# An FFT filter with a top-k FFN on one Trainium2 core: DRAM input and output padded to 128 partitions, one transfer per half

## The chip, the cores and the metric

The kernel runs on one core of one Trainium2 chip. The metric is device time in microseconds (us), the median of several executions. The core has five instruction streams: TensorE (PE in the profile, its weight loads PEld), VectorE (DVE), ScalarE (ACT), GpSimd (POOL) and SyncE (SP). In this kernel SyncE issues all plain transfers between DRAM and SBUF, and GpSimd the indirect ones (gather and scatter by a list of row numbers); 16 DMA engines carry both.

## The reference, cut to what matters

```python
# x: (8, 3136, 256) float32; filt_r, filt_i: (1569, 256); capacity C = 128
X = np.fft.rfft(x, axis=1)
y = np.fft.irfft(X * (filt_r + 1j * filt_i)[None], n=3136, axis=1)   # global filter over the sequence
scores = np.einsum('bsd,d->bs', y, w_gate)
out = y.copy()
for b in range(8):
    top = np.argpartition(-scores[b], C)[:C]          # the C tokens with the highest score
    ye = np.maximum(y[b, top] @ w1, 0.0) @ w2         # 256 -> 1024 -> 256
    out[b, top] = y[b, top] + sigmoid(scores[b, top])[:, None] * ye
```

## The kernel before

The sequence of S = 3136 tokens is split as 98 x 32, and the FFT of one batch is done in stages of matrix products. The **outer** stage reads X, a tile of [128 partitions, 2 halves, 2, 16, 128 channels], 32 KB per partition. A half is 128 of the 256 channels. The 98 rows of 32 tokens lie on partitions 0 to 48 and 64 to 112 (NH = 49 rows each), 16 tokens in each of the two blocks k of a partition. Compute instructions run over partitions 0 to 112 (113 of them); rows 49 to 63 carry nothing of use, and partitions 113 to 127 are touched by none.

For batch `b_in` the outer stage takes eight chunks of 32 channels: `fold` (L489) forms sum and difference of the two blocks, or the chunk goes in unfolded; `amm` (L500) multiplies on TensorE; `tout` (L505, VectorE) transposes the result into UU. The **inner** stage does seven steps per batch: `zmm` (L376), the products with the filter `pmul`, `qdir`, `qmul` (L384, L391, L387), `vmm` (L400), copies back to UU (L408, L410) and the scores (`gmul`, `gsum`, `gate`: L435, L441, L416). Then the outer stage of the *next* round transforms the chunk of `b_out` back (`tin` L479, `imm` or `ymm` L531, L563) and writes it into the same place of X, either with one ACT copy (`yout`, L567) or with two copies and two `join`s (L537, L541), of which the first writes the block k = 0 and the second k = 1.

**X exists once.** Round t of `outer` works on b_out = t - 1 and b_in = t + 1: a chunk of X is read as input of b_in and then overwritten with the output of b_out. After the fourth and the eighth chunk `stored` (L571) has SyncE store the half (`store_rows`), and then `load` (L584) fetches the same half for two batches on. Batch 0 is loaded in quarters (`load_first`, L602). The transfers are these:

- a store of a half (L579, L580): four transfers of 48 partitions x 16 tokens x 512 bytes, one per block k (called h there) and per half of the partitions (g), and after each two a transfer of 2 partitions for row 48;
- a load of a half (L594, L595): one of partition 112 alone, cut into 16 pieces of 1 KB, then one of partitions 0 to 111, 16 KB each. `kernel()` lays the input out in DRAM for this.

The output in DRAM is (8, 3136, 256) in the order of the tokens; a half of a token is 512 bytes and a token 1 KB.

**Selection and FFN.** `select` finds the 128 highest scores of a batch by a search in steps on ACT, TensorE and VectorE; it sends the scores to a DRAM scratch (`scr`, L672) and back spread over partitions (`R`, L698). Its step `c12` (L876) writes the row numbers `idx` for the gather from the output (`gather`, L970). `ffn` multiplies (L976 transposes, L999 and L1006 up, L1039 down), adds (`gated`, L1042) and writes back (`scatter`, L1046). w1 and w2 are loaded late (L923, L925). The FFN of the last batches is the end of the kernel.

**Order.** Every instruction stream runs in the order written out by hand in ORDER: a list of all steps, issued one after the other, so each engine takes its instructions in that order. The change leaves the list as it is.

Of the kernel before, what the change touches and what calls it, by code (L numbers as in the profile page):

```python
# [9 lines left out]
F32 = mybir.dt.float32  # L10
# [4 lines left out]
ALU = mybir.AluOpType  # L15
# [36 lines left out]
def _tables(C):  # L52
# [25 lines left out]
    k = (k1[:, None, :] + N1 * np.arange(K2)[None, :, None]).reshape(2 * K2, L)  # L78
    rows = np.minimum(k, S - k)

    cst = np.zeros((128, NCONST), f)
    p = np.arange(128)
# [11 lines left out]
    j = p // NCHK  # L94
    cst[:, _COLS["nb0"]] = (2.0**31 - j * STEPS[0] + STEPS[3] / 2)[:, None]
    cst[:, _COLS["nb1"]] = (-j * STEPS[4] + STEPS[7] / 2)[:, None]
    for r in range(8):
        d = j * (STEPS[r] - (STEPS[r + 1] if r % 4 < 3 else 0)) - (STEPS[r] / 2 if r % 4 == 3 else 0)
# [3 lines left out]
    cst[:, _COLS["half7"]] = NCHK * W7 - 2 * C + 1  # L102
    cst[:, _COLS["pick"]] = (p[:, None] % NCHK == p[None, :] % NCHK) & (p[:, None] < NROW * NCHK)
    cst[:, _COLS["block"]] = p[:, None] // NCHK == np.arange(NROW)[None, :]
    cst[:, _COLS["slot"]] = p[:, None]
    cst[:, _COLS["row"]] = N2 * p[:, None]


    tf = np.stack([tf[h, :, :, :, :, h] for h in range(2)]).reshape(128, L, 64)
# [119 lines left out]
        a=['vzaaazav', 'zazyzava', 'yyavyavv', 'avyvyaya', 'vvzayzza', 'vvavvyay', 'vaayvyvz', 'vayavyay'],  # L229
# [25 lines left out]
def kernel(  # L255
# [7 lines left out]
    nc = tc.nc  # L263
# [11 lines left out]
    HD = D // 2  # L275
    CW = 16
    DW = 2 * CW
    DS = D + 1
    oi = out.rearrange("b (h a g n) d -> b g a h n d", h=2, g=2, n=NG)
    of = out.rearrange("b s d -> (b s) d")  # L280

    c_sb = const.tile([128, NCONST], F32, name="c_sb")
    cc = {k: c_sb[:, v] for k, v in _COLS.items()}
# [8 lines left out]
    X = const.tile([128, 2, 2, NG, HD], F32, name="X")  # L292
    wg_sb = const.tile([128, D], F32, name="wg_sb")
    idx_sb = const.tile([128, B], I32, name="idx_sb")
    g_sb = const.tile([128, B], F32, name="g_sb")
# [161 lines left out]
    halves = [c_sb[:, _COLS["wi"].start + NH * k:_COLS["wi"].start + NH * k + 64] for k in range(2)]  # L457
# [115 lines left out]
            stored(c, hx)  # L573

    def store_rows(b, x):
        d = slice(x * HD, x * HD + HD)
        for h in range(2):
            for g in range(2):
                nc.sync.dma_start(out=oi[b, g, :48, h, :, d], in_=X[64 * g:64 * g + 48, x, h])  # L579
            nc.sync.dma_start(out=oi[b, :, 48, h, :, d], in_=X[48::64, x, h])  # L580

    XM = 2 * 112 * 4096

    def load(when, b, h, xy, bias=0.0):  # L584
        n = NCH // 2
        where[:] = "ld", b, h
        if b < B:
            keys = [("x", h, c, g) for c in range(h * n, h * n + n) for g in range(2)]
            to = X[:, h].rearrange("p k n d -> p (k n d)")
            main = x[b, :XM].rearrange("(h p e) -> h p e", h=2, p=112)  # L590
            ends = x[b, XM:].rearrange("(r h e) -> h r e", h=2, r=16)

            def fetch():
                nc.sync.dma_start(out=to[112:113].rearrange("p (r e) -> p r e", r=16), in_=ends[h:h + 1])  # L594
                nc.sync.dma_start(out=to[:112], in_=main[h])  # L595

            op(when, "sp", 7.15, fetch, [], keys, lat=2.2, bias=bias, tag="load")

    x_flat = X.rearrange("p x k n d -> p (x k n d)")
    x_first = x_flat.rearrange("p (q k n d) -> p q k n d", q=4, k=2, n=NG)  # L600

    def load_first():  # L602
        main = x[0, :XM].rearrange("(q p e) -> q p e", q=4, p=112)
        ends = x[0, XM:].rearrange("(r q e) -> q r e", q=4, r=16)

        def quarter(q):
            to = x_flat[:, 2048 * q:2048 * q + 2048]
            nc.sync.dma_start(out=to[112:113].rearrange("p (r e) -> p r e", r=16), in_=ends[q:q + 1])
            nc.sync.dma_start(out=to[:112], in_=main[q])

        for q in range(4):
            keys = [("x", q // 2, 4 * q + c, g) for c in range(4) for g in range(2)]
            op(XQ[q], "sp", 3.7, lambda q=q: quarter(q), [], keys, lat=2)

    def select(T0, b, st):
# [27 lines left out]
        def s1():  # L643
            st["Dt"] = Dt = sel.tile([N1, 2 * N2 + 1], F32, name="Dt")
            sp = st["sp"]
            nc.vector.tensor_reduce(out=Dt[:, N2:2 * N2], in_=sp[:N1, :, 192:224].rearrange("p g n -> p n g"), op=ALU.add, axis=AX.X)
            nc.vector.tensor_copy(out=Dt[:, 2 * N2:], in_=cc["row"][:N1])


        def s2():  # L650
# [23 lines left out]
        def s6p():  # L674

            st["ks"] = ks = flt.tile([128, 2, 2 * D], F32, name="q", bufs=BUFS["q"])[:NROW * NCHK, :, :W7]
            nc.gpsimd.memset(ks[96:], 0.0)
            nc.gpsimd.memset(ks[96:, :, W7 - N2:], -2.0**32)

        def s6q(ph):  # L680
            nc.vector.tensor_tensor(out=st["ks"][:N1, ph].rearrange("p (i n) -> p i n", n=N2), op=ALU.mult,
                                    in0=st["kf"][:, ph:ph + 1].to_broadcast([N1, NROW, N2]),
                                    in1=cc["block"][:N1, :, None].to_broadcast([N1, NROW, N2]))
# [189 lines left out]
        def c12():  # L873
            rp, col = st["rp"], st["col"]
            st["idx"] = idx = idx_sb[:, b:b + 1]
            nc.vector.tensor_scalar(out=idx[:C], in0=col[:C], scalar1=rp[:C, 2 * N2:2 * N2 + 1], scalar2=float(b * S),  # L876
                                    op0=ALU.add, op1=ALU.add)
            jk = sel.tile([128, N2], F32, name="jk")
            st["g"] = g = g_sb[:, b:b + 1]
            nc.vector.scalar_tensor_tensor(out=jk[:C], in0=cc["iota"][:C, :N2], scalar=col[:C],  # L880
                                           in1=rp[:C, N2:2 * N2], op0=ALU.is_equal, op1=ALU.mult, accum_out=g[:C])
# [77 lines left out]
    def ffn(TG, T, TE, bs, sts, plain=False):  # L959

        g = len(bs)
        where[:] = "ff", bs[0]
        one = plain or bs[0] == B - 1
        xe = [xes[b][0] for b in bs]
# [2 lines left out]
        ftile = bank  # L967

        def gather(j):
            nc.gpsimd.indirect_dma_start(out=xe[j][:C], out_offset=None, in_=of[:(bs[j] + 1) * S],  # L970
                                         in_offset=bass.IndirectOffsetOnAxis(ap=sts[bs[j]]["idx"][:C, 0:1], axis=0))

        def turn(j, ring):
# [69 lines left out]
                                           op0=ALU.mult, op1=ALU.add)  # L1043

        def scatter(j):
            nc.gpsimd.indirect_dma_start(out=of[:(bs[j] + 1) * S],  # L1046
                                         out_offset=bass.IndirectOffsetOnAxis(ap=sts[bs[j]]["idx"][:C, 0:1], axis=0),
                                         in_=xe[j][:C], in_offset=None)

# [16 lines left out]
        for f in fs:  # L1066
# [4 lines left out]
            r = XT + ([("w1",)] if one else [("wl", n) for n in range(4)])  # L1071
            op(t, "pe", cost, lambda f=f, ring=ring: up(f, 0, ring), [*r, ("ups",), *([] if one else [("u0",)])], [("uo", n0), UB] + ([("ups",)] if f == 0 else []) + ([M] if f else []), new=None if f else M)
            op(t + .1, "pe", cost, lambda f=f, ring=ring: up(f, 1, ring), r + ([("ups",)] if f == fs[-1] else []), [UB] + ([("ups",)] if f == fs[-1] else []))
            n = 4 if one else g
# [7 lines left out]
            for n, (j, q) in enumerate(parts):  # L1082
                first, final = f == q == 0, f == fs[-1] and q == (3 if one else 0)
# [82 lines left out]
    for i in range(len(PARTS)):  # L1166
        n = PARTS[i][1] - PARTS[i][0]
# [16 lines left out]
    for h in range(2):  # L1184
        load(TS + TC0 * NCH / 2 * (h + 1) + 1, 1, h, xys[1], XA)
# [59 lines left out]
```

## Time and profile before

| | |
|---|---|
| median of 3 runs | 459.41 us (453.93 to 1026.87) |
| the profiled execution | 455.47 us |
| its span, first to last instruction | 453.7 us |
| mean granted TensorE clock | 0.972 |
| moved by DMA | 69.05 MB; HBM read 41.27, written 26.91 |

The profile is of one execution. Times are us from the start of the span, unless marked ns. "Busy" is the share of the span in which an engine ran instructions; matmuls are pipelined and their ends are modelled. A line such as `[2.11 <-DMA X<-in_x_dram]` says that the engine stood idle 2.11 us before this instruction and what was seen to end that. [...]

### The profile page before, as it was taken

How to read it: one execution, taken by the hardware profiler on the slowest of the kernel's cores; microseconds unless marked ns; L12 is line 12 of the kernel's file. 1: busy time of each engine (PE TensorE's matmuls, PEld its weight loads, DVE VectorE, ACT ScalarE, POOL GpSimd, SP SyncE). 2: the span in 40 equal slices, each digit the busy share in tenths (PEclk: the TensorE clock that was granted, in tenths of full speed). 3: DMA queues.
4: the chain of work that ended last, by engine and by line, in shares of the span. 5: the costliest groups of instructions: out<-in, count | busy, mean ns of one | idle time of the engine just before them, and what ended most of it. 6: DMA issues, size and time to landing. Idle time of an engine off the chain costs nothing.

```text
span 453.7 us, 13314 instructions
## 1 busy us (share of the span) xinstructions
PE 416.2 (92%) x5348; PEld 249.7 (55%) x5348; DVE 355.8 (78%) x711; ACT 313.0 (69%) x798; POOL 328.2 (72%) x215
## 2 busy tenths in 40 slices
PE   9999999999699998979999799989999979998884
PEld 9644565545354644535555454456545756577773
DVE  2568899989869898995889698979899985964421
ACT  1429947789268977984989397948988997852210
POOL 2317799797969588867998589539889995964121
PEclk9999999999889999997999899989999989999999
DMA  8999973058654757584747563675253791566100
GB/s 230 256 258 277 243 175 92 8 138 226 163 124 111 207 136 201 144 211 110 212 103 196 152 200 91 183 183 161 63 125 96 181 267 27 131 154 151 39 25 35
DMA packets 61548, 69.05 MB, mean 152 GB/s; under 512 B 4014, under 2 KB 57550, under 8 KB 59214
## 3 DMA queue, kind: packets, MB, share of 16 engines
q1 hardware_dynamic: 60718, 66.10, 57.0%
q0 software_dynamic: 768, 2.10, 1.5%
q8 instruction: 42, 0.69, 0.6%
q14 instruction: 20, 0.16, 0.1%
HBM read 41.27 MB, written 26.91 MB: 150 GB/s over the span
## 4 chain that ended last, share of the span: by engine, by line
PE 42%; DMA 18%; DVE 15%; POOL 10%; ACT 9%; issue 4%; SPq 1%; POOLq 0%; ACTq 0%; DVEq 0%
DMA X<-in_x_dram 9%; PE pv L500 4%; DVE t L479 4%; ACT junk L441 4%; POOL q L435 3%; DMA fb_sb<-in_fri_dram 3%; PE pv L1006 3%; DVE y L384 3%; POOL xh L489 3%; PE py L400 3%; PE pa L500 3%; DMA out_dram<-X 2%; DVE q L391 2%; PE pa L1034 2%; DVE UU L505 2%
## 5 line engine op out<-in xcount | busy, mean ns | idle before, releaser
L435 POOL TENSOR_TENSOR q<-UU,wg_sb 128x1024 f32<-128x1024 f32 (+1 forms) x47 | 109.1, 2327 | 11.7 <-ACT UU L408 5.0
L541 POOL TENSOR_TENSOR X<-xh,X 113x512 f32<-113x512 f32 x64 | 81.7, 1287 | 18.5 <-ACT X L537 14.1
L441 ACT ACTIVATE junk<-q 128x256 bf16<-128x256 f32 x180 | 75.1, 417 | 13.2 <-POOL q L435 8.1
L479 DVE STREAM_TRANSPOSE t<-UU 128x1024 f32<-128x1024 f32 x64 | 78.0, 1224 | 0.0
L489 POOL TENSOR_TENSOR xh<-X 113x512 f32<-113x512 f32 x26 | 34.7, 1341 | 24.1 <-DMA X<-in_x_dram 24.1
L387 POOL TENSOR_TENSOR q<-q,fb_sb 128x1024 f32<-128x1024 f32 (+1 forms) x18 | 40.6, 2254 | 11.9 <-ACT q L380 11.7
L489 POOL TENSOR_TENSOR X<-X 113x512 f32<-113x512 f32 x24 | 31.2, 1302 | 13.2 <-DMA fa_sb<-in_fri_dram 7.0
L500 PE MATMUL pv<-X,c_sb 49*64 49x512 f32 x184 | 33.7, 709 | 7.1 <-DMA X<-in_x_dram 4.0
L441 ACT ACTIVATION_READ_ACCUMULATOR junk<-q 128x1 f32 x180 | 33.9, 188 | 0.0
L726 ACT ACTIVATE junk<-R,nb 128x392 bf16<-128x392 f32 (+1 forms) x48 | 30.0, 626 | 4.9 <-DVE nb L747 4.2
L505 DVE STREAM_TRANSPOSE UU<-pv 128x1024 f32<-128x1024 f32 x19 | 23.6, 1240 | 10.0 <-PE pv L500 9.9
L500 PE MATMUL pa<-X,c_sb 49*64 49x512 f32 x192 | 30.0, 596 | 0.5 <-DVE UU L505 0.5
L505 DVE STREAM_TRANSPOSE UU<-pa 128x1024 f32<-128x1024 f32 x21 | 25.9, 1233 | 5.4 <-PE pa L500 5.4
L1018 ACT ACTIVATE q<-pv 128x384 fp32r<-128x384 f32 (+2 forms) x18 | 8.0, 457 | 29.8 <-PE pv L1006 21.3
L1020 DVE SCALAR_TENSOR_TENSOR y<-pv,q 128x384 fp32r<-128x384 f32 (+2 forms) x18 | 9.0, 511 | 24.3 <-ACT q L1018 19.3
L384 DVE TENSOR_TENSOR y<-pa,fa_sb 128x1024 f32<-128x1024 f32 (+1 forms) x19 | 22.5, 1186 | 3.8 <-PE pa L376 2.9
L500 PE MATMUL py<-X,c_sb 49*64 49x512 f32 x168 | 24.0, 592 | 0.0
L563 PE MATMUL pz<-t,c_sb 64*64 64x512 f32 x160 | 23.1, 618 | 0.5 <-ACT X L567 0.5
L400 PE MATMUL py<-y,ti_sb 64*64 64x256 f32 x252 | 21.7, 396 | 0.7 <-DVE y L384 0.7
L376 PE MATMUL pa<-UU,tf_sb 64*64 64x256 f32 x292 | 21.2, 395 | 0.9 <-DMA tf_sb<-in_tf_dram 0.2
L400 PE MATMUL py<-q,ti_sb 64*64 64x256 f32 x252 | 21.1, 386 | 0.0
L1046 POOL DMA_INDIRECT out_dram<-fb_sb,idx_sb x6 | 5.9, 980 | 20.3 <-DVE fb_sb L1042 12.9
(340 smaller groups left out, 1144.8 us busy)
## 6 DMA issues: line engine op xcount, KB each, us to landing
X<-in_x_dram SPq DMA_DIRECT2D x14, 1792.0 KB
out_dram<-X SPq DMA_DIRECT2D x64, 384.0 KB
X<-in_x_dram SPq DMA_DIRECT2D x4, 896.0 KB
R<-scr SPq DMA_DIRECT2D x14, 196.0 KB
fb_sb<-in_moe_w_dram SPq DMA_DIRECT2D x2, 1024.0 KB
fa_sb<-in_fri_dram SPq DMA_DIRECT2D x4, 256.0 KB
fb_sb<-in_fri_dram SPq DMA_DIRECT2D x4, 256.0 KB
ti_sb<-in_ti_dram SPq DMA_DIRECT2D x1, 576.0 KB
```

The costliest lines, as they stand in the source:

```text
L384: nc.vector.tensor_tensor(out=wide(y), in0=wide(h["z"]), in1=filt(fa_sb), op=ALU.mult)
L387: nc.gpsimd.tensor_tensor(out=wide(h["q"]), in0=wide(h["q"]), in1=filt(fb_sb), op=ALU.mult)
L400: nc.tensor.matmul(v[o, j, c], lhsT=ti_at[p, k, 2 * i + e, hi], rhs=y[p, hi, c], start=k == 0, stop=k == 1)
L435: nc.gpsimd.tensor_tensor(out=h["q"][:, e0:e0 + ne].rearrange("p e (j d) -> p e j d", j=2), in0=u.rearrange("p e d j -> p e j d"), in1=wg_ ...
L441: nc.scalar.activation(out=rk, in_=h["q"][:, e, j * D:j * D + D], func=AF.Copy, accum_out=urow(b, ls[2 * e + j], D, DS))
L479: nc.vector.transpose(out=h["t"].rearrange("p d (l j) -> p d l j", j=2), in_=uchan(b_out, c))
L489: eng.tensor_tensor(out=(area(1) if k else h["f"])[:64 + NH], in0=area(0)[:64 + NH], in1=area(1)[:64 + NH], op=(ALU.add, ALU.subtract)[k])
L500: nc.tensor.matmul(ap[64 * k:64 * k + 64, g].rearrange("p (n d) -> p n d", d=DW), lhsT=todo[k][i][0][p], rhs=todo[k][i][1][p], start=i == ...
L505: nc.vector.transpose(out=uchan(b_in, c), in_=a.rearrange("p (l j) d -> p d l j", j=2))
L541: eng.tensor_tensor(out=area(k)[:64 + NH], in0=h["e"][:64 + NH], in1=odd, op=(ALU.add, ALU.subtract)[k])
L563: nc.tensor.matmul(h["y"][64 * g:64 * g + 64, k], lhsT=halves[k][p], rhs=h["t"][p, :, NG * g:NG * g + NG], start=turn == 0, stop=turn == 1)
L726: nc.scalar.activation(out=junk, in_=st["R"][:, ph], func=AF.Sign, bias=st["nb"], accum_out=cnt)
```

## The change

The input is padded with zero rows in DRAM so that a half of a batch is 128 partitions of 16 KB, and one transfer loads it; the quarters of batch 0 likewise. The output in DRAM becomes (8, 4096, 256): partition p owns 32 consecutive token rows of 1 KB, 16 for each block k, so a half is stored by one transfer of 128 partitions, with 512 bytes for each token; the padding rows are stored too, and the host picks the 3136 real tokens out and reorders them. The row numbers for gather and scatter follow the new layout: the constant `row` changes, the batch's offset is added where `Dt` is made, and in `c12` one VectorE instruction becomes two (a token of block 1 lies 64 x 32 - 16 rows further on than its column says). No compute on X, no tile and no order changes.

```diff
-    cst[:, _COLS["row"]] = N2 * p[:, None]
+    cst[:, _COLS["row"]] = (N2 * (p % NH) + NG * (p // NH))[:, None]
...
     def store_rows(b, x):
-        d = slice(x * HD, x * HD + HD)
-        for h in range(2):
-            for g in range(2):
-                nc.sync.dma_start(out=oi[b, g, :48, h, :, d], in_=X[64 * g:64 * g + 48, x, h])
-            nc.sync.dma_start(out=oi[b, :, 48, h, :, d], in_=X[48::64, x, h])
-
-    XM = 2 * 112 * 4096
+        to = out[b].rearrange("(p r) d -> p r d", p=128)[:, :, x * HD:x * HD + HD]
+        nc.sync.dma_start(out=to, in_=X[:, x].rearrange("p k n d -> p (k n) d"))
...
-            main = x[b, :XM].rearrange("(h p e) -> h p e", h=2, p=112)
-            ends = x[b, XM:].rearrange("(r h e) -> h r e", h=2, r=16)
+            main = x[b].rearrange("(h p e) -> h p e", h=2, p=128)
...
             def fetch():
-                nc.sync.dma_start(out=to[112:113].rearrange("p (r e) -> p r e", r=16), in_=ends[h:h + 1])
-                nc.sync.dma_start(out=to[:112], in_=main[h])
+                nc.sync.dma_start(out=to, in_=main[h])
...
         def quarter(q):
-            to = x_flat[:, 2048 * q:2048 * q + 2048]
-            nc.sync.dma_start(out=to[112:113].rearrange("p (r e) -> p r e", r=16), in_=ends[q:q + 1])
-            nc.sync.dma_start(out=to[:112], in_=main[q])
+            nc.sync.dma_start(out=x_flat[:, 2048 * q:2048 * q + 2048], in_=main[q])
...
-            nc.vector.tensor_copy(out=Dt[:, 2 * N2:], in_=cc["row"][:N1])
+            nc.vector.tensor_scalar(out=Dt[:, 2 * N2:], in0=cc["row"][:N1], scalar1=float(b * ROWS), scalar2=None, op0=ALU.add)
...
         def c12():
-            nc.vector.tensor_scalar(out=idx[:C], in0=col[:C], scalar1=rp[:C, 2 * N2:2 * N2 + 1], scalar2=float(b * S),
-                                    op0=ALU.add, op1=ALU.add)
+            nc.vector.tensor_scalar(out=g_sb[:C, b:b + 1], in0=col[:C], scalar1=float(NG), scalar2=float((64 - 1) * N2 + NG), op0=ALU.is_ge, op1=ALU.mult)
+            nc.vector.scalar_tensor_tensor(out=idx[:C, :1], in0=g_sb[:C, b:b + 1], scalar=col[:C], in1=rp[:C, 2 * N2:2 * N2 + 1], op0=ALU.add, op1=ALU.add)
...
-            nc.gpsimd.indirect_dma_start(out=xe[j][:C], out_offset=None, in_=of[:(bs[j] + 1) * S],
+            nc.gpsimd.indirect_dma_start(out=xe[j][:C], out_offset=None, in_=of[:(bs[j] + 1) * ROWS],
...
-    args.append(nc.dram_tensor("out_0_dram", (B, S, D), F32, kind="ExternalOutput").ap())
+    args.append(nc.dram_tensor("out_0_dram", (B, ROWS, D // 1), F32, kind="ExternalOutput").ap())
```

ROWS is 4096; the scatter changes as the gather does.

## Rows read from the trace of the kernel before

**Rows 1.** The page, busy time of each engine and its share

```profile
PE 416.2 (92%) x5348; PEld 249.7 (55%) x5348; DVE 355.8 (78%) x711; ACT 313.0 (69%) x798; POOL 328.2 (72%) x215
```

**Rows 2.** Chain that ended last, in order of time: start us, us, what

```profile
40.43 13.90 DMA X<-in_x_dram
...
144.53 6.12 DMA out_dram<-X
150.71 9.13 DMA X<-in_x_dram
...
193.53 9.98 DMA X<-in_x_dram
```

**Rows 3.** SyncE's timeline: start us, us, engine line operation, count

```profile
230.87 0.91 SPq L579 DMA_DIRECT2D out_dram<-X  x2
...
236.34 2.14 SPq L580 DMA_DIRECT2D out_dram<-X  x1
242.10 0.59 SPq L594 DMA_DIRECT2D X<-in_x_dram  x1
242.87 0.43 SPq L595 DMA_DIRECT2D X<-in_x_dram  x1
```

**Rows 4.** Timelines of GpSimd and TensorE where half 0 of X lands

```profile
159.97 1.27 POOL L489 TENSOR_TENSOR xh<-X 113x512 f32<-113x512 f32 x1 [2.97 <-DMA X<-in_x_dram]
...
203.65 2.84 PE L500 MATMUL pv<-X,c_sb 49*64 49x512 f32 x12 [2.11 <-DMA X<-in_x_dram]
...
253.15 1.28 POOL L489 TENSOR_TENSOR xh<-X 113x512 f32<-113x512 f32 x1 [4.17 <-DMA X<-in_x_dram]
253.15 2.32 PE L500 MATMUL pv<-X,c_sb 49*64 49x512 f32 x16 [3.15 <-DVE vs L631]
...
298.16 2.85 PE L500 MATMUL pv<-X,c_sb 49*64 49x512 f32 x13 [1.88 <-DMA X<-in_x_dram]
```

**Rows 5.** Windows: stretch, length, engines' busy us, granted clock, DMA share, GB/s

```profile
203.65:210.45 6.80, 6.80 (x48) 2.87 (x52) 2.77 (x6) 2.66 (x8) 6.18 (x5) 0.52 0.73 176
...
254.85:258.25 3.40, 3.40 (x36) 2.42 (x32) 1.25 (x1) 0.00 (x0) 3.27 (x2) 0.54 0.56 141
299.20:302.60 3.40, 3.40 (x40) 1.97 (x33) 1.93 (x3) 0.00 (x0) 1.48 (x2) 0.53 0.77 180
```

**Rows 6.** DMA issues: tile, queue, operation, count, KB of each

```profile
X<-in_x_dram SPq DMA_DIRECT2D x14, 1792.0 KB
out_dram<-X SPq DMA_DIRECT2D x64, 384.0 KB
...
out_dram<-X SPq DMA_DIRECT2D x32, 16.0 KB
...
X<-in_x_dram SPq DMA_DIRECT2D x14, 16.0 KB
```

**Rows 7.** Windows: a load alone, a store, its best stretch, w1's load

```profile
104.50:107.50 3.00, 2.25 (x32) 1.02 (x32) 3.00 (x4) 2.94 (x11) 2.57 (x3) 1.00 1.03 268
384.00:393.50 9.50, 9.21 (x99) 5.52 (x97) 8.25 (x29) 7.92 (x22) 9.32 (x9) 1.00 0.78 184
...
388.00:391.50 3.50, 3.50 (x49) 1.93 (x48) 3.39 (x13) 2.62 (x7) 3.47 (x4) 1.00 0.92 225
...
345.45:347.70 2.25, 2.21 (x48) 1.24 (x41) 2.14 (x9) 2.22 (x5) 2.17 (x3) 1.00 0.97 391
```

**Rows 8.** Timelines around the last store: GpSimd, SyncE, VectorE, GpSimd, TensorE

```profile
410.11 3.90 POOL L541 TENSOR_TENSOR X<-xh,X 113x512 f32<-113x512 f32 x3
...
411.44 0.89 SPq L579 DMA_DIRECT2D out_dram<-X  x2
...
422.58 0.22 DVE L876 TENSOR_SCALAR idx_sb<-col,pz 128x1 int32<-128x1 f32 x1
...
423.67 0.96 POOL L970 DMA_INDIRECT fb_sb<-out_dram,idx_sb  x1 [9.65 <-PE pv L1006]
...
432.90 0.38 PE L976 MATMUL pz<-c_sb,fb_sb 128*128 128x128 f32 x2
```

**Rows 9.** Windows: the start-up, columns as in rows 5

```profile
1.50:54.00 52.50, 51.41 (x678) 33.52 (x676) 34.58 (x40) 28.76 (x32) 23.43 (x15) 1.00 1.01 258
```

More of the change, by code (lines that the diff above doesn't have):

```diff
@@ L25 @@
 NROW = 13
+ROWS = 4096
 CUT = 2
@@ L278 @@
     DS = D + 1
-    oi = out.rearrange("b (h a g n) d -> b g a h n d", h=2, g=2, n=NG)
     of = out.rearrange("b s d -> (b s) d")
@@ L602, in load_first @@
     def load_first():
-        main = x[0, :XM].rearrange("(q p e) -> q p e", q=4, p=112)
-        ends = x[0, XM:].rearrange("(r q e) -> q r e", q=4, r=16)
+        main = x[0].rearrange("(q p e) -> q p e", q=4, p=128)
         def quarter(q):
-            to = x_flat[:, 2048 * q:2048 * q + 2048]
-            nc.sync.dma_start(out=to[112:113].rearrange("p (r e) -> p r e", r=16), in_=ends[q:q + 1])
-            nc.sync.dma_start(out=to[:112], in_=main[q])
+            nc.sync.dma_start(out=x_flat[:, 2048 * q:2048 * q + 2048], in_=main[q])
         for q in range(4):
@@ L1045, in scatter @@
         def scatter(j):
-            nc.gpsimd.indirect_dma_start(out=of[:(bs[j] + 1) * S],
+            nc.gpsimd.indirect_dma_start(out=of[:(bs[j] + 1) * ROWS],
                                          out_offset=bass.IndirectOffsetOnAxis(ap=sts[bs[j]]["idx"][:C, 0:1], axis=0),
@@ L1226 @@
     halves = rows_of.reshape(B, 2, NH, 2, NG, 2, D // 2).transpose(0, 5, 1, 2, 3, 4, 6).reshape(B, 2, 2, NH, 4096)
-    padded = np.zeros((B, 2, 64 + NH, 4096), np.float32)
-    padded[:, :, :NH], padded[:, :, 64:] = halves[:, :, 0], halves[:, :, 1]
-    first = padded[0].reshape(2, 64 + NH, 2, NG, 2, 64).transpose(0, 4, 1, 2, 3, 5).reshape(4, 64 + NH, 2048)
-    data["x"] = np.concatenate([padded[:, :, :112].reshape(B, -1), padded[:, :, 112].reshape(B, 2, 16, 256).transpose(0, 2, 1, 3).reshape(B, -1)], 1)
-    data["x"][0] = np.concatenate([first[:, :112].reshape(-1), first[:, 112].reshape(4, 16, 128).transpose(1, 0, 2).reshape(-1)])
+    padded = np.zeros((B, 2, 128, 4096), np.float32)
+    padded[:, :, :NH], padded[:, :, 64:64 + NH] = halves[:, :, 0], halves[:, :, 1]
+    data["x"] = padded.reshape(B, -1).copy()
+    data["x"][0] = padded[0].reshape(2, 128, 2, NG, 2, 64).transpose(0, 4, 1, 2, 3, 5).reshape(-1)
     data.update(fri=np.stack([np.asarray(inputs[f"filt_{x}"])[rows].reshape(64, NPR, 2, D) for x in "ri"]), tf=tf.reshape(128, -1), ti=ti, cst=cst)
@@ L1243 @@
     r = run_bass_kernel_spmd(nc, [arrays], core_ids=[0])
-    return r.results[0]["out_0_dram"]
+    rows_out = r.results[0]["out_0_dram"].reshape(B, 2, 64, 2, NG, D)[:, :, :NH]
+    return rows_out.transpose(0, 3, 2, 1, 4, 5).reshape(B, S, D)
```

## The prediction

> **What bounds the kernel now.** I read the engine table of the page first. TensorE is busy for 92% of the span and no other engine for more than 78% [rows 1]. That looks like a TensorE kernel, but such a share says nothing about why the other 8% are idle, so the chain of waits comes next. The reader is to see there that between stretches of engine work stand long single pieces called `X<-in_x_dram`: loads of 9 to 14 us for which nothing else was the last thing missing, and ahead of one of them a store, `out_dram<-X` [rows 2].
>
> The third view, SyncE's own timeline, shows what these pieces are. X is a single buffer: a half of it is written by the inverse transform, stored, and only then loaded with the next batch. For one half the store is issued at 230.87 us, the first instruction of the load at 242.10, the main load at 242.87 [rows 3], and the engines that need it go on at 253.15 [rows 4]: a round trip of 22.3 us, of which 11.2 is the store, 0.8 the load's extra end piece, 10.3 the load. The fourth view, the engines' timelines at the landings of half 0, shows who pays: GpSimd stood 2.97 us before 159.97, TensorE 2.11 us before 203.65, 3.15 before 253.15 and 1.88 before 298.16 [rows 4]. (At 253.15 the view names VectorE's `vs`, but GpSimd starts in the same instant on the X landing, so the load is what came last.) [...] So in the middle of the kernel the X round trip sets the pace once per batch.
>
> **The change, part by part.** *Bytes.* A store of a half goes from 4 x 384 + 2 x 16 KB [rows 6] = 1.606 MB to 2048 KB = 2.097 MB, a load from 1792 KB plus its 16 KB end piece = 1.851 MB to 2.097 MB. At an unchanged rate that only costs.
>
> *Rates.* They need not stay, because the shape changes, and the trace holds a transfer of the new shape. The old main load has 112 partitions and runs at 268 GB/s with the DMA engines 1.03 busy; the load of w1 has 128 partitions of 4 KB pieces and runs at 391 GB/s at 0.97 [rows 7]. The same busy engines move 1.46 times the bytes, so a piece of the old load holds its engine longer than its bytes need. The new load is 128 partitions with long contiguous pieces like w1's, so I take 391 GB/s: data time 1.851/0.268 = 6.9 us becomes 2.097/0.391 = 5.4, -1.5 us. The other bound is the old rate: 2.097/0.268 = 7.8, +0.9 us.
>
> The store has 512-byte pieces before and after, 3136 then 4096 of them, and no row shows such pieces over 128 partitions. Its bounds: the mean over the old store, 184 GB/s, gives 11.4 us against the 9.5 us that the old data takes (384.0 to 393.5 us), +1.9; w1's rate gives 5.4, -4.1. In its best stretch the old store runs at 225 GB/s with the engines 0.92 busy [rows 7]: 0.92 x 16 x 512/225 = 33.5 ns of an engine per piece. w1 spends 0.97 x 16 x 4096/391 = 163 ns on 4 KB, 20 ns per 512 bytes. The new store is like the one in piece size and like the other in partitions, so I take the middle, 27 ns, 303 GB/s with full engines: 7.0 us, -2.5 us. It will also lose the dips, since the two-partition transfers between the large ones go.
>
> [...]
>
> *SyncE's instructions.* Six issues per half store become one; the old ones hold SyncE from 230.87 to 238.48 (236.34 + 2.14) [rows 3]. The load's end piece goes: from 242.10 to 242.87, -0.8 us in front of every main load. What stands behind the store on SyncE is the scr and R transfers of the selection and the next load; the load waits for the store to land anyway and the selection gains, which I count at nothing.
>
> *The wait that is added.* The old store began with the even rows (k = 0) of a half, the new one needs all its chunks. Where a half ends in one ACT copy (half 0 of batches 1 to 4) both are ready together: 0. Where it ends in two GpSimd joins the start moves by at most one, 3.90/3 = 1.3 us (at 410.11 [rows 8]). The last store then starts at 414.0 instead of 411.4; with 8.7 us it lands near 423, as its gather issues at 423.67, and even at 13.1 us the gather would be some 3.4 us late. It transposes at 432.90 [rows 8], over 9 us after the issue. Covered; uncovered it would cost those 3.4 us.
>
> *Selection.* One more VectorE instruction per batch in c12, of the kind of L876 at 0.22 us [rows 8], eight in all. Seven lie beside VectorE work in other batches; the last lies before the same covered gather. 0 to 0.3 us; I take 0. Compute keeps its 113 partitions, so padding costs the engines nothing.
>
> **The sum.** Per round trip: -2.5 (store) - 0.8 (end piece) - 1.5 (load) = -4.8 us; bounds -4.1 - 0.8 - 1.5 = -6.4 and +1.9 - 0.8 + 0.9 = +2.0. With -4.8 the four stalls of half 0 are all shorter than the gain and go: 3.0 + 2.1 + 3.2 + 1.9 = 10.2 us, plus the 6.4 us of lost clock = 16.6. Not all of it arrives: the instruction order is fixed, VectorE is at 78% and will be the next thing that is late. I take three fifths, 10.0 us, a choice; the bounds are all and none.
>
> Start-up: from 1.5 to 54 us the DMA engines are full (1.01, 258 GB/s [rows 9]), and the chain there is a load of X [rows 2]. X makes 7.4 MB of it (batches 0 and 1, four halves of 1.851 MB): 27.6 us at 268 GB/s, then 8.39 MB at 391 = 21.5 us, -6.1 (old rate: +3.7). SyncE's issues there also wait for folds that read X, so I take half, -3.0.
>
> The profiled execution took 455.47 us; 455.5 - 10.0 - 3.0 = **442.5 us**. The runs shown have a median of 459.41, 0.9% above it, and a lowest of 453.93, 0.3% below; I sum against the profiled one.
>
> **Rivals.** *A, the forecast*: round trip about 5 us shorter, stalls gone, 442.5; its own range 433 (all 16.6 and 6.1 arrive) to 449 (half).
>
> *B, the round trip is shorter but something else is as late*: at each landing an engine finds VectorE or ACT not ready. For it: TensorE 92%, VectorE 78% [rows 1], a fixed order made for the old times. Against it: at 253.15 and 298.16 two engines waited for the same load. Then only the start-up gain and a quarter of the stalls arrive: 455.5 - 3 - 4 = 448 to 452, about 450.
>
> *C, slower: the rates stay and the bytes rise.* Place: the four half-0 round trips and the start-up. It decides from the point where the store runs under 224 GB/s (2.097 MB in 9.4 us, which with the load's +0.9 eats the 0.8 saved). For it: the old store never held more than 225 over a long stretch. Against: w1's 391 [rows 7]. Price: 4 x 2.0 + 3.7 = 12 us at its worst, 467; about half of that, 461, when the store alone gets rid of its dips.
>
> [...]
>
> *D, no change*: store and load change with opposite signs, within 1 us per round trip: 453 to 457.
>
> **Chances.** A 0.60, B 0.18, C 0.14, D 0.08. Range: 433 to 461, which leaves out the fast end of A and the slow half of C. A's own range is 433 to 449. About 2% is what a measurement of this kernel can tell from no change. Faster by over 2% (under 446 against the profiled run) takes most of A and little of B: 0.56. Slower by over 2%: nearly half of C and little else, with doubt about the median: 0.10. Within 2%: 0.34.
>
> **What would show it.** In the profile after: one store issue of 2048 KB per half; from its issue to the next load's under 9.5 us (before 11.2), the load from issue to use under 8.7 (10.3); DMA rate over 270 GB/s in stretches with a store alone and near 390 in a load alone; GpSimd's and TensorE's waits on `X<-in_x_dram` in the middle near nothing, and no stretches of low clock right behind these landings; X of batch 1 used before 51 us instead of 54.5. Wrong would be: store stretches at 225 GB/s or less (C), or faster transfers with TensorE idle as long as before in front of another releaser (B).

## The result, and the profile after

The change takes the kernel from a median of 459.6 us to 436.9 us (436.5 to 437.0): a ratio of 0.954 with a 95% interval of 0.946 to 0.963. The profiled execution took 437.0 us, its span 435.2 us, against 455.47 and 453.7 before: 18.5 us less. The forecast was 442.5, 13 us less. Medians count every execution, while the ratios, here and below, leave out those over 1.5% above the fastest of the same kernel.

The page of the kernel after: busy time per engine, the granted clock in 40 slices (tenths of full speed), shares of the chain that ended last, and of the DMA issues the loads of a half with the median us from issue to landing.

```profile
PE 406.6 (93%) x5348; PEld 242.0 (56%) x5348; DVE 360.6 (83%) x719; ACT 313.2 (72%) x798; POOL 328.3 (75%) x215
...
PEclk9999999999999999999999999999999999999999
...
PE 42%; DVE 30%; ACT 12%; POOL 8%; issue 7%; DMA 1%; POOLq 0%; ACTq 0%; DVEq 0%
...
X<-in_x_dram SPq DMA_DIRECT2D x14, 2048.0 KB, 8.0
```

The clock and the chain's shares of the kernel before, which did not stand among the rows ahead of the prediction:

```profile
PEclk9999999999889999997999899989999989999999
...
PE 42%; DMA 18%; DVE 15%; POOL 10%; ACT 9%; issue 4%; SPq 1%; POOLq 0%; ACTq 0%; DVEq 0%
```

DMA was 18% of the chain before and is 1% after; VectorE went from 15% to 30% and is now the second part of the chain. The slices of lower clock are gone, and TensorE's busy time fell by 9.6 us with the same 5348 matmuls [rows 1].

**The transfers.** SyncE's timeline of the kernel after, at the landing that [rows 3] shows for before: one store issue, then the load.

```profile
221.05 0.57 SPq L577 DMA_DIRECT2D out_dram<-X  x1
230.21 0.33 SPq L588 DMA_DIRECT2D X<-in_x_dram  x1
```

From the store's issue to the load's are 9.2 us, where [rows 3] has 11.2 to the end piece and 12.0 to the main load. At the five stores of half 0 from 89 to 288 us of before, SyncE's timelines give, to the main load's issue, 12.2, 10.8, 10.9, 12.0 and 10.9 us before, 9.6, 10.2, 9.4, 9.2 and 9.2 after: 1.9 us less in the mean. Windows of the kernel after, columns as in [rows 5]: the store's data, a load's data, the same load from the issue above in steps of a microsecond, and the start-up.

```profile
223.00:229.00 6.00, 6.00 (x92) 3.12 (x86) 5.76 (x9) 4.85 (x16) 6.00 (x5) 1.00 0.95 290
...
190.40:193.40 3.00, 3.00 (x56) 1.63 (x48) 2.93 (x8) 2.87 (x12) 2.42 (x1) 1.00 1.01 429
...
235.00:236.00 1.00, 1.00 (x29) 0.69 (x25) 1.00 (x3) 0.85 (x3) 1.00 (x1) 1.00 1.03 442
...
237.00:238.00 1.00, 0.83 (x24) 0.46 (x16) 1.00 (x2) 0.91 (x4) 1.00 (x1) 1.00 0.12 33
...
1.50:50.00 48.50, 47.12 (x602) 31.43 (x600) 30.79 (x34) 24.09 (x23) 19.34 (x13) 1.00 0.94 308
```

The store runs at 290 GB/s where the old one had 184 over its length and 225 at its best [rows 7], the load at 429 where the old one had 268. The load issued at 230.21 is all but over after 237 (33 GB/s) and lands 8.2 us after its issue, at 238.4.

**The landings.** GpSimd's timeline, where half 0 lands:

```profile
155.24 1.29 POOL L489 TENSOR_TENSOR xh<-X 113x512 f32<-113x512 f32 x1 [2.08 <-DMA X<-in_x_dram]
...
239.42 1.30 POOL L489 TENSOR_TENSOR xh<-X 113x512 f32<-113x512 f32 x1
```

TensorE's timeline at the three landings at which it stood before [rows 4]:

```profile
196.70 1.93 PE L500 MATMUL pv<-X,c_sb 49*64 49x512 f32 x16
...
240.35 1.90 PE L500 MATMUL pv<-X,c_sb 49*64 49x512 f32 x16
...
281.87 1.96 PE L500 MATMUL pv<-X,c_sb 49*64 49x512 f32 x16
```

No bracket stands behind the three: TensorE did not wait. The load of the second landed at 238.4 and is first read at 239.42, so it now has about a microsecond to spare, and the next thing to be late is an engine.

**Where the time went.** Both kernels issue the same matmuls in the same order, so the start of one and the same matmul can be compared in the two traces. Between two places the difference moves by a step; the forecast of the same step stands beside it, worked out from the prediction's terms (stall, and the lost clock behind it).

```
place (us, before)             step measured   in the prediction
start-up, to 85 us                  +0.5         -3.0
121: selection, then low clock      -4.7         not there
160: GpSimd's stall                 -0.5         -3.0
203.65: TensorE's stall             -5.2         -5.4  (2.1 + 0.48 x 6.8)
253.15                              -4.9         -4.7  (3.15 + 0.46 x 3.4)
298.16                              -3.4         -3.5  (1.9 + 0.47 x 3.4)
370: wait for w2                    -3.6         not there
403: VectorE, given back            +1.9         not there
rest, slow drift                    +1.4
sum                                -18.5
three fifths of the stalls                      -10.0; with the start-up -13.0
```

### The profile page after: what moved, and what is told of

It is laid out like the page before. It is cut to its first block, busy times and chain, and to the rows that moved or that the text cites. A ratio compares the mean times of both kernels' runs of the same rounds, so it can differ in the third digit from the quotient of the medians.

```text
span 435.2 us, 13093 instructions
## 1 busy us (share of the span) xinstructions
PE 406.6 (93%) x5348; PEld 242.0 (56%) x5348; DVE 360.6 (83%) x719; ACT 313.2 (72%) x798; POOL 328.3 (75%) x215
## 4 chain that ended last, share of the span: by engine, by line
PE 42%; DVE 30%; ACT 12%; POOL 8%; issue 7%; DMA 1%; POOLq 0%; ACTq 0%; DVEq 0%
DVE t L479 6%; ACT junk L441 5%; DVE y L384 5%; DVE UU L505 5%; DVE q L391 4%; POOL q L435 4%; PE pa L500 3%; PE py L500 3%; PE pv L996 3%; PE pv L400 2%; PE py L1108 2%; PE py L400 2%; PE pa L1024 2%; PE py L989 2%; PE py L1115 2%
## 5 line engine op out<-in xcount | busy, mean ns | idle before, releaser
L435 POOL TENSOR_TENSOR q<-UU,wg_sb 128x1024 f32<-128x1024 f32 (+1 forms) x47 | 109.9, 2345 | 10.4 <-ACT UU L408 6.0
L541 POOL TENSOR_TENSOR X<-xh,X 113x512 f32<-113x512 f32 x64 | 82.0, 1292 | 14.4 <-ACT X L537 10.4
L441 ACT ACTIVATE junk<-q 128x256 bf16<-128x256 f32 x180 | 75.1, 417 | 10.3 <-POOL q L435 5.6
L489 POOL TENSOR_TENSOR xh<-X 113x512 f32<-113x512 f32 x26 | 33.6, 1299 | 9.8 <-DMA X<-in_x_dram 9.8
L500 PE MATMUL pv<-X,c_sb 49*64 49x512 f32 x184 | 28.8, 594 | 0.0
L563 PE MATMUL pz<-t,c_sb 64*64 64x512 f32 x160 | 22.2, 595 | 0.2 <-ACT X L567 0.2
L400 PE MATMUL py<-y,ti_sb 64*64 64x256 f32 x252 | 20.7, 380 | 0.7 <-DVE y L384 0.7
## 6 DMA issues: line engine op xcount, KB each, us to landing
ti_sb<-in_ti_dram SPq DMA_DIRECT2D x1, 576.0 KB, 10.6
```

What stands on the lines that cost most here:

```text
L400: nc.tensor.matmul(v[o, j, c], lhsT=ti_at[p, k, 2 * i + e, hi], rhs=y[p, hi, c], start=k == 0, stop=k == 1)
L435: nc.gpsimd.tensor_tensor(out=h["q"][:, e0:e0 + ne].rearrange("p e (j d) -> p e j d", j=2), in0=u.rearrange("p e d j -> p e j d"), in1=wg_ ...
L441: nc.scalar.activation(out=rk, in_=h["q"][:, e, j * D:j * D + D], func=AF.Copy, accum_out=urow(b, ls[2 * e + j], D, DS))
L489: eng.tensor_tensor(out=(area(1) if k else h["f"])[:64 + NH], in0=area(0)[:64 + NH], in1=area(1)[:64 + NH], op=(ALU.add, ALU.subtract)[k])
L500: nc.tensor.matmul(ap[64 * k:64 * k + 64, g].rearrange("p (n d) -> p n d", d=DW), lhsT=todo[k][i][0][p], rhs=todo[k][i][1][p], start=i == ...
L541: eng.tensor_tensor(out=area(k)[:64 + NH], in0=h["e"][:64 + NH], in1=odd, op=(ALU.add, ALU.subtract)[k])
```

## The experiments

Each median below stands against runs of the kernel before on the same chip in the same session; ratios are to that one. "Later by" compares the same matmul with the kernel after.

### The new loads alone, the old store

```diff
 load, load_first, kernel(): as after
 def store_rows(b, x): as before (six transfers)
```

> The input is padded and loaded in one transfer of 128 partitions, the store and the output stay as before. Theory (half 0's round trip sets the pace once per batch): the load loses its end piece, 0.8 us, and about 2 us of data time, so that the round trip is some 3 us shorter; the stalls of 2 to 3 us at the landings of half 0 then nearly vanish, and with them the stretches of low clock: 442 to 448 us. Rival (the six issues of a store on SyncE held things up, not the data): no more than 2 us are gained, 453 to 457 us.

Measured: 437.2 us (435.4 to 442.1), ratio 0.956 [0.947, 0.964]. The loads alone bring nearly all of the gain, more than the 442 to 448 that I expected. Windows of this kernel, first a load, then a store:

```profile
192.50:195.50 3.00, 2.88 (x48) 1.48 (x44) 2.87 (x12) 2.90 (x10) 1.72 (x1) 1.00 0.96 410
...
181.00:188.00 7.00, 6.28 (x104) 3.52 (x100) 6.32 (x12) 6.26 (x19) 5.80 (x5) 1.00 0.80 186
```

Its store still runs at 186 GB/s, in six transfers (issue to load's issue 10.6 us), and only TensorE's low stretch of 3.4 us near 121 stays: 1.7 us are lost there against after. That stretch is no work of the old store, since the control below has it with the fast one, and 1.6 us are lost there too. So at the landings neither the six issues on SyncE nor the slow store alone costs the kernel its time, once the load is fast.

### The new store alone, the old loads

The store needs partitions 113 to 127 to hold something; in the first form they are filled once, during batch 1's load, in the second behind batch 2's.

```diff
 load, load_first, kernel(): as before, and, once:
+                if b == 2 and h == 1:
+                    nc.sync.dma_start(out=X[113:128].rearrange("p x k n d -> p (x k n d)"), in_=x[1, :15 * 8192].rearrange("(p e) -> p e", p=15))
```

> The output is padded and stored in one transfer of 128 partitions, the loads stay as before (112 partitions and the end piece); 15 unused partitions of X are filled once in the load of batch 1. Theory: the store's data takes 7.2 us instead of 9.5, the round trip is some 2 us shorter, the stalls at the landings shrink but do not all vanish, and some low clock stays: 443 to 450 us. If the SyncE issues were the cause, this kernel has the whole gain: 436 to 439 us.

The first form: 452.0 us (447.4 to 459.0), ratio 0.990 [0.986, 0.994], over the 443 to 450 expected. Its fill delays the start-up by 10.4 us at 69 us, so it doesn't answer the question.

> The store alone once more, with the 15 unused partitions of X filled at a time when the DMA engines are idle (behind the second load of batch 2) and not in the crowded start. In the first run of the store alone the start-up, up to 69 us, was 10.4 us later than in the changed kernel, and only 6.8 us were lost after it. Theory: without the fill in the start the store alone keeps most of the gain: 440 to 446 us. Rival (the loads alone matter, the store gives nothing): 450 to 453 us again.

The second form: 447.7 us (443.1 to 452.5), ratio 0.983 [0.970, 0.996], between the two ranges expected. By the profiled executions it loses 7.5 us to the kernel after behind the start-up (later by 2 us there), so it keeps about three fifths of the gain; by the ratios, 1.7% against 4.6%, it is under two fifths. One load of it:

```profile
196.50:201.50 5.00, 4.55 (x72) 2.34 (x71) 4.79 (x16) 4.87 (x14) 2.86 (x3) 1.00 0.97 295
```

The two halves of the change are not additive: each shortens the same round trip, and once that is short enough the rest of the other's gain is slack. On top of the new loads the new store changes the median by less than can be told (437.2 and 436.9 us, from two sessions).

### The store over 64 partitions twice, and a control with two transfers over 128

This changes the partitions that one transfer spans and nothing else: the same bytes, the same pieces of 512 bytes. The control has two transfers as well, but each over all 128 partitions, one per block k.

```diff
 64 partitions:
-        nc.sync.dma_start(out=to, in_=X[:, x].rearrange("p k n d -> p (k n) d"))
+        for g in range(2):
+            nc.sync.dma_start(out=to[64 * g:64 * g + 64], in_=X[64 * g:64 * g + 64, x].rearrange("p k n d -> p (k n) d"))
 control:
+        for k in range(2):
+            nc.sync.dma_start(out=to[:, NG * k:NG * k + NG], in_=X[:, x, k])
```

> As the changed kernel, but each store is two transfers, partitions 0 to 63 and then 64 to 127; bytes and 512-byte pieces stay. Theory (the rate hangs on how many partitions a transfer spans, both halves or one): while one of them runs alone the rate falls from 290 to about 220 GB/s, the store takes 9.5 us of data or a little less, and some of the stalls come back: 438 to 445 us. Rival (what counts is the number and size of pieces, or the small end transfers that went): 290 GB/s as before, 436 to 438 us.

> The control to the store in two transfers of 64 partitions: again two transfers of 1 MB for each store, again 512-byte pieces, but each spans all 128 partitions, one for each block k. Theory (the rate hangs on the partitions a transfer spans): 290 GB/s as in the changed kernel, 436 to 439 us. Rival (two transfers in place of one are what cost): about 176 GB/s as with the two halves of the partitions, 460 to 470 us.

Measured: 468.2 us (466.2 to 469.2), ratio 1.025 [1.018, 1.033], for 64 partitions; 436.8 us (436.8 to 437.7), 0.965 [0.954, 0.977], for the control. A store's window and SyncE's timeline with 64 partitions:

```profile
236.00:246.00 10.00, 9.93 (x146) 5.43 (x140) 9.80 (x18) 8.76 (x28) 9.43 (x7) 1.00 0.80 187
...
233.81 3.35 SPq L578 DMA_DIRECT2D out_dram<-X  x2
247.09 0.33 SPq L589 DMA_DIRECT2D X<-in_x_dram  x1
```

The same two views of the control:

```profile
223.00:229.00 6.00, 6.00 (x92) 3.39 (x88) 5.21 (x8) 4.85 (x15) 6.00 (x5) 1.00 0.96 286
...
221.59 2.27 SPq L578 DMA_DIRECT2D out_dram<-X  x2
230.56 0.35 SPq L589 DMA_DIRECT2D X<-in_x_dram  x1
```

187 against 286 GB/s, 13.3 against 9.0 us to the load. In this kernel the number of transfers, one or two, costs nothing; the partitions that one of them spans decide the rate. Two transfers over the two halves of the partitions do not add up to the rate of one over both. With 13.3 us the old stalls are back (GpSimd waits 17.4 us for X in all and TensorE 8.9) and the low clock behind them too, at 205, 257 and 304 us among others: 7, 8 and 8 tenths in the page's slices of 11.7 us there. I had expected 438 to 445: I had counted the later store and not that it would again reach an engine, which costs the clock as well. No run shows the 220 GB/s of that expectation: [rows 7] has 225 in the old store's best stretch, and here 187 was measured.

The control also has the wait at 119 us and the low clock at 121 of which the section on the prediction speaks; TensorE's timeline and a window:

```profile
119.31 0.30 PE L804 MATMUL pa<-rc,c_sb 64*64 64x2 f32 x7 [1.96 <-DVE ge L786]
...
121.70:125.10 3.40, 3.40 (x22) 1.72 (x18) 2.91 (x10) 2.95 (x9) 3.05 (x2) 0.50 0.76 313
```

### The load over 112 partitions

```diff
 first form, in two pieces:
-                nc.sync.dma_start(out=to, in_=main[h])
+                nc.sync.dma_start(out=to[112:], in_=main[h, 112:])
+                nc.sync.dma_start(out=to[:112], in_=main[h, :112])
 second form, from batch 3 on only:
+                    nc.sync.dma_start(out=to[:112], in_=main[h, :112])
```

In the second form partition 112, row 48 of the second 49, is not loaded from batch 3 on.

> As the changed kernel, but the loads of batches 1 to 7 are two transfers, partitions 112 to 127 and then 0 to 111, with the same bytes and the same 16 KB pieces. Theory (112 partitions are spread badly over the engines): the large one runs at about 268 GB/s instead of 400, the load takes about 3 us longer, stalls at half 0's landings come back in part: 440 to 447 us. Rival (the rate came from padding, that is from contiguous 2 MB in DRAM, or the end piece of 1 KB pieces was the cost): about 400 GB/s, 437 to 439 us.

> As the changed kernel, but from batch 3 on the load takes partitions 0 to 111 only: one transfer, one issue, 12% fewer bytes; row 48 of the second 49 rows is left out of the input. Theory (the rate hangs on the partitions a transfer spans and how they fall on the engines): 1.84 MB at about 280 GB/s take 6.6 us instead of 5.1, and 440 to 445 us follow although fewer bytes move. Rival (bytes at a constant rate): 4.5 us of data, 435 to 437 us.

The first form: 455.8 us (453.3 to 461.6), ratio 1.002 [0.998, 1.007], the whole gain gone, where 440 to 447 was expected. But it holds two things, the 112 partitions and a small transfer ahead of them, and 5.5 us of what is lost stand in the start-up. The page of this kernel, its two loads with the median us from issue to landing:

```profile
X<-in_x_dram SPq DMA_DIRECT2D x14, 1792.0 KB, 10.8
...
X<-in_x_dram SPq DMA_DIRECT2D x14, 256.0 KB, 4.3
```

The second form leaves one of the two things: 438.4 us (437.8 to 439.5), ratio 0.966 [0.958, 0.974], between the two ranges expected, so that its time alone decides nothing. Windows of its loads:

```profile
190.30:193.30 3.00, 3.00 (x48) 1.42 (x44) 2.93 (x8) 2.90 (x10) 2.62 (x2) 1.00 0.90 251
...
234.00:239.00 5.00, 5.00 (x72) 2.55 (x68) 4.86 (x13) 4.31 (x12) 4.62 (x4) 1.00 0.99 305
```

The page of this second kernel, its loads of 112 partitions:

```profile
X<-in_x_dram SPq DMA_DIRECT2D x10, 1792.0 KB, 9.1
```

An eighth fewer bytes land no earlier: 9.1 us after the issue, where loads of 128 partitions have 8.0 in the kernel after, and 7.8 to 8.8 in the others whose pages give it. The data move at 251 to 305 GB/s where those have 429. So 112 partitions are the slow shape, and padding to 128 pays for its own bytes; the 16 extra rows are not what costs.

In time this shape costs little here. From its start-up to its end the second form loses 2.9 us to the kernel after, and 1.7 of them at 121 us, where the control of the store loses 1.6 with the fast load. The microsecond to spare at a landing takes up most of the rest. What costs more is a small transfer ahead of the load. With it the load of 112 partitions lands 10.8 us after its issue instead of 9.1 (first form), and behind the old end piece 9.8 (the new store alone, 447.7 us). I had not set out to separate the two, and no run has the end piece ahead of 128 partitions; but by these kernels most of what the new load brings comes from the transfer that went, and not from the sixteen partitions.

### Half 0's load made longer

```diff
+                if h == 0 and b >= 3:
+                    nc.sync.dma_start(out=to[:, 2048:], in_=main[h, :, 2048:])
                 nc.sync.dma_start(out=to, in_=main[h])
```

From batch 3 on the load of half 0 is preceded by 1 MB of the same data again, and is issued 5.0 to 5.9 us later for it.

> As the changed kernel, but in front of each load of half 0 from batch 3 on, half of its bytes are loaded once more (128 partitions, 8 KB each), so that the round trip of half 0 grows by 4 to 5 us and nothing else changes. Theory (that round trip sets the pace once per batch, and low clock follows each stall): at the five landings of half 0 the stalls and the stretches of low clock come back, 448 to 456 us. Rival (the gain came from SyncE's issues or from the DMA engines being less busy): 437 to 440 us.

Measured: 471.9 us (470.8 to 472.7), ratio 1.039 [1.031, 1.048]: later by 35.7 us than the kernel after, in steps of 5.8, 7 to 7.8, 8, 7.2 and 7.4 us at the five landings. One of them in TensorE's timeline, and the window behind it:

```profile
166.54 3.69 PE L500 MATMUL pv<-X,c_sb 49*64 49x512 f32 x16 [4.98 <-DMA X<-in_x_dram]
...
166.50:173.30 6.80, 6.76 (x56) 2.43 (x56) 2.00 (x6) 1.56 (x6) 6.51 (x5) 0.50 0.72 217
```

A wait of about 5 us stands there, and low clock for 6.8 us follows at 166.5 (0.50), 214.3, 265.5 and 313.3, a further 3.4 us: 5.0 + 3.4 = 8.4, of which 7 to 8 show. The mean granted clock of this execution is 0.963, where the kernel after has 0.998. Beyond the microsecond to spare nothing covers the round trip of half 0, and of these 5.0 to 5.9 us each costs more than a microsecond. That carries the forecast's mechanism. My expected 448 to 456 counted the wait and part of the slack, and not the clock behind it.

### The idle matmuls of the start-up

Ahead of the first X matmul the kernel runs WARM = 56 matmuls on zeros (the trace counts each of them as two), and more as fillers between the first ones.

```diff
-    WARM=56
+    WARM=30
```

> As the changed kernel, but with 30 idle matmuls in front instead of 56. In the changed kernel the first X is folded by 10.3 us, yet the first matmul on it starts at 14.7, behind 9.5 us of these idle matmuls and 4.2 us of further ones. Theory (the start-up gained nothing since TensorE's fixed run of idle matmuls, not X, sets it): what follows moves 2 to 4 us earlier up to 50 us, and some of it arrives: 433 to 436 us. Rival (the start-up waits for the filter tables and the load of batch 1): 436 to 438 us, the time at 55 us unchanged.

Measured: 434.8 us (433.9 to 435.7), ratio 0.959 [0.951, 0.967]; earlier than the kernel after by 4.6 us at 57 us and by 3.1 at the end (1.6 are lost at a low stretch of 3.4 us at 117, which the control of the store has too). The chain of the kernel after, its first three steps (start, us, what):

```profile
1.00 9.49 PE py L1108 x112
10.49 4.20 PE py L1115 x72
14.69 1.02 PE pv L500 x8
```

The same of the kernel with 30:

```profile
1.00 5.07 PE py L1108 x60
6.07 4.20 PE py L1115 x72
10.27 1.02 PE pv L500 x8
```

In the kernel after, the first folds of X end at 10.25 us (VectorE's 2.34 us from 7.91), and TensorE reads them at 14.7, behind matmuls on zeros. In this kernel the start-up was bound by these and not by the load.

Two runs went on from there, with 3 instead of 6 matmuls per filler, and the second with WARM = 12:

> As the changed kernel with 30 idle matmuls in front and half of the later idle ones (three instead of six per filler). With 30 in front the first matmul on X moved from 14.7 to 10.2 us, and 3.1 us of that reached the end of the profiled run. Theory (idle matmuls still stand in the way of X): another 1 to 2 us, 432 to 435 us. Rival (X and the filter tables set the start by now): 434 to 436 us, or more where TensorE's clock falls for lack of the fillers.

> As the last one with 12 idle matmuls in front. The first fold of X ends at 10 us, so matmuls on X can't start much before that: theory, no gain over 30 in front, 432 to 436 us; if the clock rises later because less runs in front, 436 to 440 us.

434.3 us (432.6 to 437.0) and 436.5 us (434.9 to 444.7): nothing more to be had. With 12 in front, the median is in the range for a clock that rises later. The profiled execution, 444.7 us, has the granted clock at 0.50 from 9.4 to 19.6 us, where the kernels with 56 and with 30 have 1.00. And the kernel before with WARM = 30:

> The kernel before with 30 idle matmuls in front instead of 56, nothing else. My forecast had the start-up bound by the loads of X. If that held for the kernel before, shorter idle work gives nothing there: 453 to 458 us. If the idle matmuls set the start there too, it gains 2 to 4 us, about 1% under the kernel before.

450.5 us (441.9 to 456.1), ratio 0.986 [0.979, 0.992]. The ratio is in the range for idle matmuls that set part of the start there too, but no trace shows it: its runs spread widely, and its profiled one has a start 5 to 7 us later, with four loads of the filter tables (8.8 to 17.3 us each) as the first long steps of the chain. What sets that spread was not found.

The kernel after with WARM = 30 has the lowest medians of this study with its variant of 3 per filler, 434.8 and 434.3 us. They come from other sessions than the 436.9, so the 2 us between them rest on the aligned traces (3.1 us at the end), not on a paired ratio.

## Why the prediction was right, and where its steps failed

The mechanism was right (case A): the round trip of half 0 sets the pace, the new shape runs faster (loads at 429 instead of 268 GB/s, stores at 290 instead of 184), the stalls and the low clock behind them go. 436.9 us lies in A's own range of 433 to 449, and the point forecast was 5.6 us too high. That it came so near is in part luck. By the table above the four stalls of the sum gave 14.0 us instead of 10.0, two places outside the sum 8.3 more, and the start-up -0.5 instead of 3.0; 1.9 were given back, and the drift took 1.4. The steps, in the prediction's order:

- **Rates.** The load was taken at 391 GB/s and 5.4 us; in the window above it runs at 429, 4.9 us for its bytes. The store was taken at 303 GB/s and 7.0 us; it runs at 290, 7.2 us, 0.95 x 16 x 512/290 = 27 ns per piece, the middle that was chosen. (The upper bound of the store was too low: 184 GB/s over 9.5 us are 1.75 MB, more than the store's 1.606, so other transfers ran in that window.)
- **The round trip.** From the store's issue to the main load's it lost 1.9 us in the mean, forecast were 2.5 and 0.8, 3.3. The end piece was sized rightly (0.8), the store was not: 1.0 instead of 2.5. 9.2 to 10.2 us after, where under 9.5 was the sign to look for. The load lands 8.0 us after its issue (median), under the 8.7 that were the sign; its first use, at 239.42, comes 9.2 us after it, because GpSimd arrives later. Before, the four landings of [rows 4] came 9.3 to 10.3 us after the main load's issue, 9.9 in the mean. In all the round trip lost 1.9 + 1.9 = 3.8 us of the 4.8 forecast, still more than TensorE's longest stall of 3.15 [rows 4], so the error did not show in the time.
- **The three fifths.** The step that failed most. TensorE's three stalls came back whole with their clock: 5.2 + 4.9 + 3.4 = 13.5 us of 13.6 by the rows. The 6.4 us of lost clock in the sum are 0.48 x 6.8 + 0.46 x 3.4 + 0.47 x 3.4, an estimate from [rows 5] that takes the work done as in proportion to the granted clock; no run shows the 6.4 by itself, but these steps hold both parts and agree. I had feared that a VectorE busy for 78% would be late next. It is next (30% of the chain), but only after the whole stall has gone.
- **GpSimd's stall at 160.** Counted at its full 3.0, worth 0.5 to 0.8. TensorE didn't stand there, and GpSimd still waits 2.08 us after. The store ahead of this landing is also the one that gained least, from 10.8 to 10.2 us. A stall of an engine for which TensorE doesn't wait should not have stood in the sum beside TensorE's.
- **The start-up.** -3.0 forecast, +0.5 measured, though the transfers did get faster (308 GB/s at a DMA share of 0.94, where [rows 9] has 258). X of batch 1 is used at 53.97 us without a wait, not before 51. I read full DMA engines and an X load in the chain as the bound, and did not ask what TensorE does until 15 us; the kernel with WARM = 30 shows it.
- **Two places not in the sum.** At 121 us of the kernel before the same delay reaches TensorE by a detour. GpSimd's timeline, VectorE's, then TensorE's, and windows of the low clock:

```profile
111.78 1.30 POOL L489 TENSOR_TENSOR xh<-X 113x512 f32<-113x512 f32 x1 [1.81 <-DMA X<-in_x_dram]
...
117.12 2.86 DVE L489 TENSOR_TENSOR X<-X 113x512 f32<-113x512 f32 x1 [1.18 <-POOL xh L489]
...
121.47 0.42 PE L813 MATMUL pa<-rc,c_sb 64*64 64x2 f32 x8 [3.90 <-DVE ge L795]
...
370.06 4.95 PE L1034 MATMUL pa<-fb_sb 128*128 128x256 f32 x14 [2.19 <-DMA fb_sb<-in_moe_w_dram]
...
121.70:128.50 6.80, 6.38 (x60) 3.75 (x60) 4.89 (x19) 2.95 (x9) 5.21 (x3) 0.51 1.03 259
370.90:374.30 3.40, 3.40 (x10) 2.74 (x9) 1.90 (x6) 2.94 (x9) 3.38 (x4) 0.54 0.88 237
```

The bracket names VectorE's `ge`, not X. But VectorE's own timeline shows it waiting 1.18 us for GpSimd's fold (at 117.12) shortly ahead of `ge`, and the fold came late because of X. In the profiled execution after, the first wait is gone, TensorE's is 2.00 us (at 119.99), and the low clock (6.8 us from 121.7, where the clock is now 1.00) is gone: 1.9 + 3.4 = 5.3 us by these rows, 4.7 measured. That the detour is the cause is argued from this order. The new store alone keeps GpSimd's wait (1.25 us) and all of the low clock. With the new loads alone, in the control of the store, with 112 partitions alone and with WARM = 30 GpSimd's wait is gone as in the kernel after, and TensorE waits as long as there, 1.96 to 2.00 us; but 3.4 us of low clock follow in each of them (0.50 in the control's window, 8 tenths in the slice from 120 us of the new loads' page). So the shorter wait and half of the low clock go with the change; for the other half, 1.7 us, no cause is shown.

The second place is the wait at 370.06: before, TensorE waits 2.19 us for w2's load (`fb_sb`), and 3.4 us of low clock follow (from 370.9): 2.2 + 0.46 x 3.4 = 3.8 us by the rows, 3.6 measured. TensorE's timeline of the kernel after has no such wait there:

```profile
351.31 3.26 PE L1024 MATMUL pa<-fb_sb 128*128 128x256 f32 x14 [0.30 <-PE py L400]
```

SyncE's timelines, before and after, show what set it:

```profile
352.46 1.84 SPq L579 DMA_DIRECT2D out_dram<-X  x2
...
360.61 1.13 SPq L925 DMA_DIRECT2D fb_sb<-in_moe_w_dram  x1
...
335.60 1.15 SPq L577 DMA_DIRECT2D out_dram<-X  x1
336.84 5.53 SPq L915 DMA_DIRECT2D fb_sb<-in_moe_w_dram  x1
```

w2's load stands behind a store on SyncE: before, it is issued 8.2 us after that store's first transfer, after, 1.2 us behind it. With the old store and the new loads TensorE still waits 1.42 us there, with the new store and the old loads 0.30. So here the old store did cost time. The prediction put what stands behind a store on SyncE at nothing, and its sum looked at the landings of X alone.

- **What was given back.** At 403 us of before, 384.45 of after, 1.9 us are lost. VectorE's timeline of the kernel after, then GpSimd's, then TensorE's, and last VectorE's of the kernel before:

```profile
380.73 3.67 DVE L932 TENSOR_TENSOR ti_sb<-fb_sb,ti_sb 128x512 fp32r<-128x512 f32 x1
...
380.31 1.00 POOL L1036 DMA_INDIRECT out_dram<-xr,idx_sb  x1 [0.17 <-DVE ok L735]
381.34 2.50 POOL L541 TENSOR_TENSOR X<-xh,X 113x512 f32<-113x512 f32 x2
...
384.45 0.50 PE L1029 MATMUL pa<-ti_sb,q 128*128 128x256 f32 x2 [1.43 <-DVE ti_sb L932]
...
400.90 0.68 DVE L942 TENSOR_TENSOR ti_sb<-fb_sb,ti_sb 128x512 fp32r<-128x512 f32 x1
```

The same VectorE instruction took 0.68 us before, when GpSimd's sums began only after its end (at 401.73). After, they begin 0.61 us behind its start, and it ends 0.56 us after theirs (383.84), as if it had begun then. TensorE waits for it.

Of the rivals, C had the mechanism of the store run over 64 partitions: at 187 GB/s, below the 224 from which C decides, it measured 468.2 us, and C's worst was 467. So bytes alone do not set the time: 2.1 MB take 13.3 us from store to load over two halves and 9.0 over all partitions. B (something else is as late) shows in one place, the 1.9 us given back.

## What to carry to other kernels

Give each transfer all 128 partitions, even if rows have to be padded for it: here loads with a seventh more bytes landed 7.8 to 8.8 instead of 9.1 us after their issue, and stores in two halves of 64 partitions ran at 187 instead of 286 GB/s. Send no small transfer ahead of a large one that is waited for (with one, the load of 112 partitions landed 10.8 us after its issue, without 9.1). Price a stall of TensorE with the low clock behind it (2.1 us of waiting cost 5.2) and take such stalls whole, but leave out those of engines that TensorE doesn't wait for (GpSimd's 2.97 us were worth 0.5 to 0.8). Look also at what stands behind a transfer on the engine that issues it (w2's load, issued 8.2 us behind the first part of a store, made TensorE wait 2.19 us). Where a start-up looks bound by full DMA engines, see first what the first engine does until it reads its data.

## What was not expected of the hardware

- After each wait of TensorE for X shown here a stretch of granted clock of 0.50 to 0.54 follows, of 3.4 or 6.8 us: behind 2.11 us at 203.65 one of 6.8, behind 3.15 at 253.15 one of 3.4 [rows 4, 5], in the kernel with the longer load one of 6.8 behind 4.98. The length of the wait did not tell which of the two came, and not every wait brings one: none follows the 2.00 us at 119.99 in the kernel after (1.00 from 121 to 128 us), where 3.4 us follow 1.96 at 119.31 in the control.
- VectorE's sum of `fb_sb` and `ti_sb` took 3.6 to 3.7 us in ten of the fourteen profiles and 0.68 in four. In the ten, GpSimd's sums begin 0.56 to 0.61 us after it, and it ends 0.55 us behind them; in the four it has ended before they begin, or none is near. What makes it longer was not shown: no run here set out to test it.
- With a load of 16 partitions ahead of it, the load of 112 landed 10.8 us after its issue; without, 9.1.
